# Queries through the hardware queues, wider warm-up matmuls and one PSUM tile less at the start of a sorted-attention and expert-layer kernel

## The chip, the core and the metric

The kernel runs on one core of a Trainium2 chip. TensorE (PE) multiplies matrices, VectorE (DVE), ScalarE (ACT) and GpSimd (POOL) work on vectors, SyncE (SP) issues transfers. The metric is the device time of one execution in microseconds. Three runs of the kernel before gave 359.15, 359.16 and 359.26 us, with a median of 359.16.

## The reference

Inputs: queries, keys and values of shape (4 batches, 8 heads, 768 positions, 64 features); a sort net of 8x8 numbers for each batch and head; expert weights w1 (4 experts, 512x1024) and w2 (4, 1024x512) and their probabilities for 3,072 tokens.

```python
P = sort_net
for _ in range(5):                      # alternating normalization
    P = exp(P - max(P))
    P = P / (sum(P, axis=-1) + 1e-9)
    P = P / (sum(P, axis=-2) + 1e-9)
k_sorted = einsum('bhij,bhjcd->bhicd', P, k_blocks)   # 8 blocks of 96 positions, mixed
v_sorted = einsum('bhij,bhjcd->bhicd', P, v_blocks)
attn = softmax(q_block @ k_sorted_block.T / 8)        # inside each block
x = attn @ v_sorted_block                             # to (3072 tokens, 512)
p = domain_probs / (sum(domain_probs) + 1e-9)
out = sum over e of p[:, e] * (relu(x @ w1[e]) @ w2[e])
```

## The kernel before

The work is written out by hand, in the order in which each engine is to take it; nothing reorders it. PSUM tiles come from pools that hand out two buffers in turn (`psM` and `psA`), so a tile waits until the one two before it in its pool has been read.

The start, which is all that the change touches, runs as follows. SP loads the sort net (L76) and the probabilities (L163). POOL issues, one after the other, the first half of the queries of batch 0 (two loads, L147), the keys and values of batch 0 in two groups of four heads (L110, cast from float32 to float16 on the way), the first expert's w1 (L134) and, between them, builds the identity matrix and masks. A query half is 64 positions of each row group; `half_queries` names it, `q0` holds it in float16.

PE meanwhile multiplies a constant tile (`dummy`, 128x128) by itself 84 times (`warm`, L260), transposes the first queries (`h_q`, L271, 48 matmuls) and multiplies `dummy` another 30 times.

The normalization loop (L283) is a chain between two engines: ACT's Exp (L284) on 32x64 numbers, then six DVE operations (two sums, two reciprocals, two products), five times. `p_steps` is a generator that normalizes the expert probabilities on DVE; each `next(p_steps)` (L301) puts one of its steps (sum, add, reciprocal, product with transfers) into DVE's order. At the last round DVE and POOL each expand one half of the normalized matrix into `sn16` (L304).

Then PE multiplies `sn16` by the identity (`r_half`, L316) into the PSUM tile `ps_R`, giving the matrix on all partitions. DVE builds the mixing operands `PI0` from it in two steps of four heads (`build_PI0`, L327). `mix_half` (L495, 24 matmuls for four heads, half of the output blocks) mixes keys or values into its own PSUM tile, after some matmuls on `dummy` (`keep_warm`, L481); `mixed` (L506) copies it out. `h_s` computes scores and their exponentials (L550, L556), `h_w` transposes values (L522), `h_a` applies the attention (L567), `h_x` transposes the result for the expert layer (L598), and `group0` (L679) is the first expert layer on it. Work of the first four heads (quad 0) and the second four (quad 1) is interleaved from L1365 on. `Rs` (L1372) is an SBUF copy of `ps_R`. From about 20 us on, PE works through the expert layers, with attention of later batches between them, to the end.

Of the kernel before, what the change touches and what calls it, by code (L numbers as in the profile page):

```python
# [9 lines left out]
F32 = mybir.dt.float32  # L10
F16 = mybir.dt.float16
# [6 lines left out]
def kernel(  # L18
# [11 lines left out]
    nc = tc.nc  # L30

    B, H, S, D = q.shape
    GH = B * H
# [5 lines left out]
    P = 128  # L39
# [3 lines left out]
    R = BLK // CP  # L43
    NKC = Dm // P
    NFC = FF // P
    NPB = H // 2
    HB = NB // 2
# [7 lines left out]
    const = ctx.enter_context(tc.tile_pool(name="const", bufs=1))  # L55
# [3 lines left out]
    psM = openM.enter_context(tc.tile_pool(name="psM", bufs=2, space=bass.MemoryType.PSUM))  # L59
# [5 lines left out]
    state = {"n": 0, "q": 0}  # L65

    def psa(shape, dtype, name):
        state["n"] += 1
        return psA.tile(shape, dtype, tag="ps", name=name)

    def psm(shape, dtype, name):
        return psM.tile(shape, dtype, tag="ps", name=name)
# [9 lines left out]
    Hflat = Hb.rearrange("p e f x -> p (e f x)")  # L82
# [12 lines left out]
    q0 = Tt[3].rearrange("p a f x -> p (a f x)").rearrange("p (f h r d) -> p f h r d", f=2, h=4, r=R)  # L95
# [7 lines left out]
    def half_queries(qd, hf):  # L103
        return q[0, ds(4 * qd, 4)].rearrange("h (p r) d -> p h (r d)", r=R)[ds(64 * hf, 64)]

    def load_natural(b, nm, qd):
        src = {"k": k, "v": v}[nm]
        t = arena[:, ds(("k", "v").index(nm) * 2 * NW + qd * NW, NW)].rearrange("p (h r d) -> p h r d", h=4, r=R)
        natural[(b, nm, qd)] = t
        nc.gpsimd.dma_start(  # L110
            t.rearrange("p h r d -> p h (r d)"),
            src[b, ds(4 * qd, 4)].rearrange("h (p r) d -> p h (r d)", r=R),
        )
# [9 lines left out]
    def head(b, nm, h):  # L123
        return natural[(b, nm, h // 4)][:, h % 4, :, :]

    w1sb, w2sb = [], []
# [4 lines left out]
    def load_w1(e, parts=1):  # L131
        n = NKC // parts
        for i in range(parts):
            nc.gpsimd.dma_start(  # L134
                w1sb[e][:, ds(i * n, n)], moe_w1[e].rearrange("(kc p) f -> p kc f", p=P)[:, ds(i * n, n)]
            )
# [8 lines left out]
    def load_half_queries(hf):  # L145
        for qd in range(2):
            nc.gpsimd.dma_start(  # L147
                q0[ds(64 * qd, 64), hf].rearrange("p h r d -> p h (r d)"), half_queries(qd, hf)
            )

    dummy = Hflat[:, ds(2 * NFC * 2 * P, P)]
    nc.vector.memset(dummy, 0.5)


# [2 lines left out]
    def p_part(at, n):  # L157
        return Tt[2].rearrange("p a f x -> p (a f x)")[:, ds(2 * at, 2 * n)].bitcast(F32)

    p_in = p_part(0, E * NT).rearrange("p (t e) -> p t e", e=E)  # L160
    p_out = p_part(E * NT, E * NT).rearrange("p (e t) -> p e t", e=E)
    p_den = p_part(2 * E * NT, NT).rearrange("p (t o) -> p t o", o=1)
    nc.sync.dma_start(p_in, moe_domain_probs.rearrange("(p t) e -> p t e", t=NT))  # L163
    load_half_queries(0)
    load_natural(0, "k", 0)


    ident = const.tile([P, P], F16, name="ident")
    make_identity(nc, ident)
    load_natural(0, "v", 0)  # L170
    load_natural(0, "k", 1)
    load_natural(0, "v", 1)
    load_w1(0, 2)

    eye16 = const.tile([P, CP], F16, name="eye16")
    maskk = const.tile([P, P], F16, name="maskk")
# [76 lines left out]
    qTs = {}  # L253
    q_ring = const.tile([P, 3, R, P], F16, name="q_ring")

    def warm(n):
        ps = psM.tile([P, 4, P], F32, tag="ps", name=f"ps_w_{state['n']}")
        state["n"] += 1
        for m in range(n):
            nc.tensor.matmul(ps[:, m % 4, :], dummy, dummy, start=True, stop=True)  # L260

    qT0 = [from_spare(2 * S).rearrange("p (s f r x) -> p s f r x", s=2, f=2, r=R) for _ in range(2)]

# [13 lines left out]
    srow = const.tile([GH, NB, 1], F32, name="srow")  # L277
    scol = const.tile([GH, NB, 1], F32, name="scol")
    sn16 = const.tile([GH, NB, NB, CP], F16, name="sn16")
    warm(84)  # L280
    p_steps = spread_weights()
    nc.gpsimd.tensor_copy(ident6, ident[0:R, 0:R])
    for it in range(5):  # L283
        nc.scalar.activation(sn[:], sn[:], AF.Exp, bias=0.0, scale=1.0)  # L284
        if it == 4:
            for qd in range(2):
                h_q(qd, 0, nc.scalar.copy)
            warm(30)
        nc.vector.tensor_reduce(srow[:], sn[:], AX.X, ALU.add)
        nc.vector.reciprocal(srow[:], srow[:])  # L290
        nc.vector.tensor_tensor(sn[:], sn[:], srow[:].broadcast_to([GH, NB, NB]), ALU.mult)
        nc.vector.tensor_reduce(scol[:], sn[:].rearrange("p i j -> p j i"), AX.X, ALU.add)
        nc.vector.reciprocal(scol[:], scol[:])
        if it < 4:
            nc.vector.tensor_tensor(
                sn[:], sn[:],
                scol[:].rearrange("p j o -> p o j").broadcast_to([GH, NB, NB]),
                ALU.mult,
            )
            if it:  # L300
                next(p_steps)  # L301

    for a, eng in enumerate((nc.vector, nc.gpsimd)):
# [4 lines left out]
            ALU.mult,  # L308
        )

    ps_R = psM.tile([P, 2, 512], F32, tag="ps", name="ps_R")
    Rv = ps_R[:, :, 0:HB * GH].rearrange("p a (i g) -> p a i g", g=GH)

    def r_half(a):
        for i in range(HB):
            nc.tensor.matmul(  # L316
                Rv[:, a, i, :], sn16[:, a * HB + i, :, :].rearrange("g j c -> g (j c)"),
                ident[0:GH, 0:GH], start=True, stop=True,
            )
# [155 lines left out]
    xsls0, xsl0 = {}, {}  # L475
    vT0 = {qd: from_spare(S) for qd in range(2)}

    def keep_warm(ps, n):

        for _ in range(n):  # L480
            nc.tensor.matmul(ps, dummy, dummy, start=True, stop=True)  # L481

    tails = {}

    def mix_half(nm, qd, hf, pool, warm_up=0):

        ps = pool([P, 1024], F32, f"ps_m{nm}_{qd}_{hf}")
        keep_warm(ps[:, 0:P], warm_up)
        tails[(nm, qd, hf)] = ps[:, 2 * R * 64:1024].bitcast(F16).rearrange("p (n x) -> p n x", n=2)
        ps = ps[:, 0:2 * R * 64].rearrange("p (s r x) -> p s r x", s=2, r=R)  # L490
        for sg in range(2):
            for r in range(R):
                for hh in range(2):
                    h = 4 * qd + 2 * sg + hh
                    nc.tensor.matmul(  # L495
                        ps[ds(D * hh, D), sg, r, :],
                        head(0, nm, h)[:, r, :],
                        PI0[hf][:, h, :, :].rearrange("p i c -> p (i c)"),
                        start=True, stop=True,
                    )  # L500
        return ps
# [38 lines left out]
    def h_s(qd, qq, ps=None):  # L540

        kT, ET = kTs[qd], ETs[2 * qd + qq % 2]
        if ps is None:
            ps = psa([P, 2, 512], F32, f"ps_s0_{qd}_{qq}")
        for n in range(4):
            for hh in range(2):
                sg, i = n // 2, 2 * (qq % 2) + n % 2

                m = BLK if 2 * i + sg == 3 else P
                nc.tensor.matmul(  # L550
                    ps[0:m, hh, ds(n * BLK, BLK)],
                    kT[ds(D * hh, D), ds((2 * i + sg) * BLK, m)],
                    qT0[qd][ds(D * hh, D), sg, qq // 2, :, ds((2 * (qq % 2) + n % 2) * CP, CP)],
                    start=True, stop=True,
                )
        nc.scalar.activation(  # L556
            ET[:, 0:S].rearrange("c (h x) -> c h x", h=2), ps[0:BLK, :, 0:HS],
            AF.Exp, bias=0.0, scale=SCALE,
        )
# [30 lines left out]
    def h_x(qq, copy, qds=range(2), ps=None, warm_up=0):  # L590

        nq = len(qds)
        if ps is None:
            ps = psa([P, 2, 512], F32, f"ps_x0_{qq}_{qds[0]}")
        keep_warm(ps[:, 0, 0:P], warm_up)
        for m, qd in enumerate(qds):
            for n in range(4):
                nc.tensor.matmul(  # L598
                    ps[:, m, ds(n * BLK, BLK)], xsl0[(qd, qq)][:, n, :, :].rearrange("c h d -> c (h d)"),
                    perm[:], start=True, stop=True,  # L600
                )
        copy(
            xTs[0][:, :, ds(2 * qq, 2), :].rearrange("p (q s) i x -> p q s (i x)", q=2)[:, ds(qds[0], nq)],
            ps[:, 0:nq, 0:4 * BLK].rearrange("p q (s x) -> p q s x", s=2),
        )
# [55 lines left out]

    def open_group(qq, g, warm_up=0):
        ps = groups[(qq, g)] = psm([P, 2, 512], F32, f"ps_h_0_{qq}_{g}")
        keep_warm(ps[:, 0, 0:P], warm_up)

    def group0(qq, nq, g, kcs=range(NKC), later=False):

# [5 lines left out]
        if (qq, g) not in groups:  # L673
            open_group(qq, g)
# [305 lines left out]
    for e in range(E):  # L980
        w, hk, hf = w1sb[e], NKC // 2, FF // 2
# [380 lines left out]
    ]  # L1362


    mk0 = mix_half("k", 0, 0, psm, 8)  # L1365
    mixed("k", 0, mk0, 0, 2, act)
    mv0 = mix_half("v", 0, 0, psa)
    mixed("v", 0, mv0, 0, 2, vec)
    h_s(0, 0)
    r_half(1)  # L1370
    mixed("k", 0, mk0, 2, 2, act)
    vec(Rs.rearrange("p g (a i) -> p a g i", a=2), Rv.rearrange("p a i g -> p a g i"))  # L1372
# [18 lines left out]
    h_w(1, vec, 0, 2, tails[("v", 1, 0)])  # L1391
    mixed("v", 1, mv1, 2, 2, act)
    ps_a10 = psa([P, 2, 512], F32, "ps_a10")
    keep_warm(ps_a10[:, 0, 0:P], 4)
    even01 = h_a(0, 1, ps_s01, True)
    h_a(1, 0, ps_a10)
    next(p_steps)
# [138 lines left out]
```

## Time and profile before

| What | Value |
|---|---|
| Median of three runs | 359.16 us (359.15 to 359.26) |
| Span of the profiled execution, first to last instruction | 357.8 us |
| Own time of the profiled execution | not given by the page; the median is 1.36 us above its span |
| PE busy, share of the span | 351.6 us, 98% |
| DVE, ACT, POOL busy | 276.2, 170.6, 133.6 us |
| Granted TensorE clock | 1.000 |
| HBM read, written | 42.13 MB, 6.34 MB |

The profile shows one execution. A chain of waits follows the work that ended last backwards, at each step to whatever released it. "Issue" in it is time in which an engine waited for nothing that the profile shows. In a timeline each line has a start, a duration (or the stretch of a merged group), the engine, the source line, the operation, the tiles and how many instructions were merged; in brackets stands the idle time before and who ended it. PEld is PE's weight load, one for every matmul.

### The profile page before, as it was taken

The page shows a single profiled execution, that of the slowest core. Times are in us where ns is not written, and L with a number is a line of the kernel's source. Part 1 is how long each engine was busy: PE and PEld are TensorE (multiplying, and loading weights), DVE is VectorE, ACT ScalarE, POOL GpSimd, SP SyncE. Part 2 cuts the span into 40 slices and gives each one's busy share as a digit, 9 for nine tenths or more (in the row PEclk, how much of TensorE's full clock was granted, in tenths as well). Part 3 has the DMA queues.
Part 4 walks back from the last instruction along what each step waited for, and adds up shares of the span by engine and source line. Part 5 has one row for each costly group of instructions (what it writes and reads, how often), then busy time and mean ns, then how long its engine had stood idle before and what let it go on. Part 6 is the DMA issues. An engine that isn't in the chain of part 4 may idle for free.

```text
span 357.8 us, 9498 instructions
## 1 busy us (share of the span) xinstructions
PE 351.6 (98%) x3949; PEld 306.3 (86%) x3949; DVE 276.2 (77%) x552; ACT 170.6 (48%) x303; POOL 133.6 (37%) x149
## 2 busy tenths in 40 slices
PE   8899999999999999999999999999999999999996
PEld 8686867888888888888899988888888888888886
DVE  5754797869889587868978988896678886588963
ACT  2554240442434535367947258830288611688201
POOL 8864010375122222000535318840058800188400
PEclk9999999999999999999999999999999999999999
DMA  8999999999999999935996420005200015100011
GB/s 114 207 205 228 216 210 198 209 163 165 201 154 160 188 152 170 194 74 73 168 201 90 102 78 0 2 2 108 102 29 2 3 39 138 61 0 2 2 73 46
DMA packets 72022, 40.51 MB, mean 113 GB/s; under 512 B 40614, under 2 KB 66732, under 8 KB 71980
## 3 DMA queue, kind: packets, MB, share of 16 engines
q0 software_dynamic: 36576, 19.93, 41.9%
q1 hardware_dynamic: 35260, 19.92, 28.5%
q8 instruction: 31, 0.51, 0.6%
q14 instruction: 11, 0.09, 0.1%
q10 hardware_dynamic: 144, 0.07, 0.1%
HBM read 42.13 MB, written 6.34 MB: 135 GB/s over the span
## 4 chain that ended last, share of the span: by engine, by line
PE 95%; DVE 2%; ACT 1%; DMA 0%; issue 0%; DVEq 0%
PE ps_h L790 18%; PE ps_Q L1264 18%; PE ps_p L774 12%; PE ps_X L1121 10%; PE ps_Z L1121 7%; PE ps_Q L1121 7%; PE ps_Z L1264 6%; PE ps_h L679 3%; PE ps_o L714 3%; PE ps_p L830 3%; PE ps_a L453 2%; PE ps_s L418 2%; PE ps_k L399 1%; PE ps_v L365 1%; PE ps_a L567 1%; PE ps_mk L495 1%
## 5 line engine op out<-in xcount | busy, mean ns | idle before, releaser
L790 PE MATMUL ps_h<-xT,w 128*128 128x256 f16 x576 | 67.5, 273 | 0.0
L790 PEld LDWEIGHTS <-w 128*128 128x128 f16 x576 | 55.2, 98 | 7.2
L796 DVE SCALAR_TENSOR_TENSOR Hb<-ps_h,pb 128x1024 f16<-128x1024 f32 x34 | 41.5, 1223 | 17.2 <-PE ps_h L790 15.8
L1121 PEld LDWEIGHTS <-w 128*128 128x128 f16 x480 | 43.6, 98 | 4.8
L1134 POOL TENSOR_TENSOR arena<-tmp,pb 128x512 f16<-128x512 f32 x12 | 15.2, 1275 | 65.7 <-PE ps_Z L1121 49.8
L1264 PEld LDWEIGHTS <-Hb 128*128 128x128 f16 x320 | 31.1, 98 | 3.5
L1133 ACT ACTIVATE tmp<-tmp 128x512 f32<-128x512 f32 x46 | 29.0, 632 | 3.9 <-DVE tmp L1171 3.9
L1264 PEld LDWEIGHTS <-Sb 128*128 128x128 f16 x304 | 28.3, 98 | 3.0
L1121 PEld LDWEIGHTS <-arena 128*128 128x128 f16 x312 | 27.7, 98 | 2.9
L425 ACT ACTIVATE ET<-ps_s 96x768 f16<-96x768 f32 x24 | 18.0, 802 | 25.1 <-PE ps_s L418 24.8
L121 POOL DMA_DIRECT2D arena<-in_q_dram x24 | 19.9, 838 | 25.5 <-DMA q_ring<-arena 25.2
L408 ACT CAST kT<-ps_k 64x384 f16<-64x384 f32 x48 | 22.7, 473 | 13.3 <-PE ps_k L399 12.3
L1121 PE MATMUL ps_X<-ET,arena 128*128 128x256 f16 x168 | 25.2, 272 | 0.0
L1264 PE MATMUL ps_Q<-w,Hb 128*128 128x256 f16 x192 | 24.6, 273 | 0.0
L774 PEld LDWEIGHTS <-Hb 128*128 128x128 f16 x232 | 21.8, 98 | 3.0
L1127 DVE SCALAR_TENSOR_TENSOR Hb<-ps_X,pb 128x512 f16<-128x512 f32 x27 | 18.7, 691 | 7.0 <-PE ps_X L1121 7.0
L1141 ACT COPY ps_X<-ps_Z 128x512 f32<-128x512 f32 x27 | 15.4, 571 | 17.8 <-PE ps_Z L1121 17.8
L1121 PE MATMUL ps_Z<-xT,w 128*128 128x256 f16 (+1 forms) x176 | 22.5, 258 | 0.0
L760 DVE TENSOR_TENSOR Sb<-Hb 128x512 f16<-128x512 f16 x33 | 20.6, 647 | 0.0
L1148 ACT COPY tmp<-ps_X 128x512 f32<-128x512 f32 x26 | 15.2, 585 | 9.2 <-PE ps_X L1121 6.6
L1127 DVE SCALAR_TENSOR_TENSOR Hb<-ps_Z,pb 128x512 f16<-128x512 f32 x27 | 18.4, 682 | 1.3 <-PE ps_Z L1121 1.3
L1171 DVE TENSOR_TENSOR tmp<-ps_Q,tmp 128x512 f32<-128x512 f32 x26 | 17.8, 683 | 0.8 <-PE ps_Q L1121 0.8
(266 smaller groups left out, 741.6 us busy)
## 6 DMA issues: line engine op xcount, KB each, us to landing
w<-in_moe_w_dram POOLq DMA_DIRECT2D x6, 1024.0 KB, 27.9
pb<-p_dram SPq DMA_DIRECT2D x9, 512.0 KB, 7.0
arena<-in_k_dram POOLq DMA_DIRECT2D x8, 384.0 KB, 9.3
arena<-in_v_dram POOLq DMA_DIRECT2D x8, 384.0 KB, 7.5
vs<-arena SPq DMA_DIRECT2D x36, 66.0 KB, 4.9
arena<-in_q_dram POOLq DMA_DIRECT2D x24, 96.0 KB, 7.5
out_dram<-ob SPq DMA_DIRECT2D x9, 256.0 KB, 2.0
w<-in_moe_w_dram POOLq DMA_DIRECT2D x4, 512.0 KB, 12.5
```

The costliest lines, as they stand in the source:

```text
L121: nc.gpsimd.dma_start(t[:, h // 2, :, h % 2, :], q[b, h].rearrange("(t p) d -> p t d", p=P))
L408: nc.scalar.copy(kT[ds(D * hh, D), r], pk[ds(D * r, D), hh].rearrange("p a (i c) -> p a i c", c=CP),)
L425: nc.scalar.activation(ETs[2 * (pr % 2) + hh][:, 0:S].rearrange("c (a x) -> c a x", a=2), pss[hh][0:BLK, :, 0:HS], AF.Exp, bias=0.0, scale ...
L760: tt(sm[0], blk(0, 1), blk(1, 1), ALU.add)
L774: nc.tensor.matmul(ps, lhs(e, f), Ts[e][rhs][:, f, :], start=(first and e == es[0] and f == 0), stop=(done and e == es[-1] and f == KH - 1 ...
L790: nc.tensor.matmul(ps[:, f, :], w1sb[e][:, kc, ds((4 * g + f) * P, P)], xT[:, kc, ds(2 * c * P, 2 * P)], start=(kc == 0), stop=(kc == NKC ...
L796: nc.vector.scalar_tensor_tensor(out=Hb[:, homes.get(e, e), ds(4 * g, 4), :], in0=ps[:], scalar=0.0, op0=ALU.max, in1=weights(e).broadcast ...
L1121: nc.tensor.matmul(dst[:, ds(f * cols, cols)], a[lhs][:, k, ds((f0 + f) * P, P)], t[rhs][:, k, :], start=(first and f == 0 and k == 0), st ...
L1127: nc.vector.scalar_tensor_tensor(out=home(i, j), in0=src.rearrange("p (f x) -> p f x", f=m), scalar=0.0, op0=ALU.max, in1=weight(j).broadc ...
L1133: nc.scalar.activation(src, src, AF.Relu, bias=0.0, scale=1.0)
L1171: tt(t12, Q, u2, ALU.add)
L1264: nc.tensor.matmul(ps, lhs(e, f), Ts[e][rhs][:, f, part], start=(first and e == 0 and f == 0), stop=(e == E - 1 and f == KH - 1), skip_gro ...
```

## The change

Six edits are made together.

1. The first half of the queries of batch 0 is loaded as float32, one half of the heads by SP's queue and the other by ACT's, into a part of the room of the first expert's w2. ACT casts it into `q0` in two copies, in rounds 2 and 3 of the normalization loop (counted from 0), behind the Exp. POOL no longer issues these loads; the loads of keys, values and w1 come first on POOL, and the identity is made after them.
2. `dummy` has 512 columns, and a warm-up matmul multiplies its first 128 columns by all 512: 21 in place of 84, 8 in place of 30, 2 in place of 8 before the key mix, 1 in place of 4 before `ps_a10` is used.
3. `ps_R` is a tile of 1,024 columns, with the sort matrices in its last 256, and the first key mix takes the first 768 of the same tile in place of a tile of its own.
4. As `mix_half` takes no tile for that mix, later tiles of `psM` move by one buffer.
5. The first step of `p_steps` moves from round 1 to round 2, the second from 2 to 3, and the third, a reciprocal, from round 3 to behind the first `h_s`.
6. `keep_warm` is defined earlier, and `warm` calls it.

```diff
-    dummy = Hflat[:, ds(2 * NFC * 2 * P, P)]
+    dummy = Hflat[:, ds(2 * NFC * 2 * P, 512)]
...
+    q32 = w2sb[0].rearrange("p f d -> p (f d)").bitcast(F32)[:, 0:4 * R * D].rearrange("p (h x) -> p h x", h=4)
+    for qd, queue in enumerate((nc.sync, nc.scalar)):
+        queue.dma_start(q32[ds(64 * qd, 64)], half_queries(qd, 0))
     nc.sync.dma_start(p_in, moe_domain_probs.rearrange("(p t) e -> p t e", t=NT))
-    load_half_queries(0)
     load_natural(0, "k", 0)
-    ident = const.tile([P, P], F16, name="ident")
-    make_identity(nc, ident)
     load_natural(0, "v", 0)
     load_natural(0, "k", 1)
     load_natural(0, "v", 1)
     load_w1(0, 2)
+    ident = const.tile([P, P], F16, name="ident")
+    make_identity(nc, ident)
...
+    def keep_warm(ps, n):
+        for _ in range(n):
+            nc.tensor.matmul(ps, dummy[:, 0:P], dummy, start=True, stop=True)
     def warm(n):
-        ps = psM.tile([P, 4, P], F32, tag="ps", name=f"ps_w_{state['n']}")
+        ps = psM.tile([P, 512], F32, tag="ps", name=f"ps_w_{state['n']}")
         state["n"] += 1
-        for m in range(n):
-            nc.tensor.matmul(ps[:, m % 4, :], dummy, dummy, start=True, stop=True)
+        keep_warm(ps[:], n)
...
-    warm(84)
+    warm(21)
     for it in range(5):
         nc.scalar.activation(sn[:], sn[:], AF.Exp, bias=0.0, scale=1.0)
+        if it in (2, 3):
+            nc.scalar.copy(
+                q0[:, 0, ds(2 * (it - 2), 2)].rearrange("p h r d -> p h (r d)"), q32[:, ds(2 * (it - 2), 2)]
+            )
         if it == 4:
             for qd in range(2):
                 h_q(qd, 0, nc.scalar.copy)
-            warm(30)
+            warm(8)
...
-            if it:
+            if it > 1:
                 next(p_steps)
...
-    ps_R = psM.tile([P, 2, 512], F32, tag="ps", name="ps_R")
-    Rv = ps_R[:, :, 0:HB * GH].rearrange("p a (i g) -> p a i g", g=GH)
+    ps_R = psM.tile([P, 1024], F32, tag="ps", name="ps_R")
+    Rv = ps_R[:, 2 * R * 64:1024].rearrange("p (a i g) -> p a i g", a=2, g=GH)
...
-    def mix_half(nm, qd, hf, pool, warm_up=0):
-        ps = pool([P, 1024], F32, f"ps_m{nm}_{qd}_{hf}")
-        keep_warm(ps[:, 0:P], warm_up)
+    def mix_half(nm, qd, hf, pool, warm_up=0, ps=None):
+        if ps is None:
+            ps = pool([P, 1024], F32, f"ps_m{nm}_{qd}_{hf}")
+        keep_warm(ps[:, 0:512], warm_up)
...
-    mk0 = mix_half("k", 0, 0, psm, 8)
+    mk0 = mix_half("k", 0, 0, psm, 2, ps_R)
     mixed("k", 0, mk0, 0, 2, act)
     mv0 = mix_half("v", 0, 0, psa)
     mixed("v", 0, mv0, 0, 2, vec)
     h_s(0, 0)
+    next(p_steps)
     r_half(1)
...
-    keep_warm(ps_a10[:, 0, 0:P], 4)
+    keep_warm(ps_a10[:, 0, :], 1)
```

## The prediction

> **What bounds the kernel now.** I read the page's engine line, queues and chain first, then the chain of waits and the timeline of the first 32 us, which the change touches.
>
> ```profile
> span 357.8 us, 9498 instructions
> PE 351.6 (98%) x3949; PEld 306.3 (86%) x3949; DVE 276.2 (77%) x552; ACT 170.6 (48%) x303; POOL 133.6 (37%) x149
> ...
> q8 instruction: 31, 0.51, 0.6%
> ...
> PE 95%; DVE 2%; ACT 1%; DMA 0%; issue 0%; DVEq 0%
> ```
>
> TensorE (PE) carries 95% of the chain. Nothing in the diff alters its real work, so only a shift of the moment when it becomes continuously busy counts. The chain of waits of the start (start, us, what):
>
> ```profile
> 0.74 1.71 DMA sn<-in_sort_net_dram
> ...
> 2.47 0.27 ACT sn L284
> ...
> 11.06 0.69 DVE sn L304
> ...
> 12.64 0.58 PE ps_mk L495 x24
> ...
> 13.99 0.18 issue
> ...
> 14.73 0.43 DVE Rs L1372
> ...
> 18.95 0.40 PE ps_a L567 x8
> ...
> 20.07 0.20 issue
> ```
>
> The sort net's load starts five rounds of Exp (ACT) and six DVE operations, 1.77 us a round; TensorE's warm-up and the loads lie beside them. From 11.79 the chain runs through PE, ACT and DVE in turn, and from 20.3 it stays on PE. Two "issue" pieces stand in it. The timeline shows them as stops inside a group of equal matmuls, where no engine is waited for:
>
> ```profile
> 9.43 0.28 DVE L235 RECIPROCAL T<-T 128x24 f32<-128x24 f32 x1
> 12.17 0.75 DVE L327 TENSOR_TENSOR Sb<-maskk,ps_R 128x256 f16<-128x256 f16 x2 [0.43 <-PE ps_R L316]
> 13.78 0.21 PE L550 MATMUL ps_s<-Sb,kT 64*128 64x96 f16 x1 [0.19 <-ACT kT L506]
> 14.17 0.33 PE L550 MATMUL ps_s<-Sb,kT 64*128 64x96 f16 x7 [0.18 <-issue]
> 17.50 0.35 PE L550 MATMUL ps_s<-Sb,kT 64*128 64x96 f16 x8
> 19.85 0.22 PE L522 MATMUL ps_s<-ident,Sb 128*96 128x128 f16 x1
> 20.27 0.37 PE L522 MATMUL ps_s<-ident,Sb 128*96 128x128 f16 x3 [0.20 <-issue]
> ```
>
> Each of these matmuls started about 0.4 us after the one before (13.78 to 14.17, 19.85 to 20.27). Counting weight load and matmul pairs in the timeline from the start (84, 48, 30, 4, 8, 24, 24, ...), the stops fall at the 224th and the 352nd pair: 128 pairs, or 256 instructions, apart. The instruction queue moved 31 packets of 0.51 MB in all, 16 KB each, and PE's 7,898 instructions make 31 blocks of 256. So I read the stops as PE reaching a block that had not arrived. The DMA view has refills starting at 11.79, 17.86 and 23.89 us, each 2.4 us before such a block is used (14.17, 20.27); the block after 20.27 follows 6.1 us behind the one before.
>
> **The change, part by part.**
>
> *Start.* ScalarE now issues a query load ahead of its table load. SyncE's two first loads were issued 0.47 us apart, so the table load moves from 0.74 to 1.21 and ends at 2.49, against the Exp's start at 2.47: +0.04. The two query loads also share the DMA engines with the sort net's last packets: between 0 and 0.25 us (three of the 84 ns that a 2,048 B packet of the hardware queue takes in the trace). A gain is excluded, since the sort net's landing sets the start. I take +0.1 for both, with ends 0 and 0.3, near the low end because the probabilities' 48 KB, right behind the sort net, landed in 1.8 us beside its 1.7.
>
> *Query loads and casts.* POOL loses two query issues (1.4 us), so key, value and w1 issues and the masks come earlier; nothing waits for them today (masks done by 9.9, used at 12.17). Two casts of 128x768 enter ScalarE behind the third and fourth Exp (6.02, 7.78). The row of 128x768 casts from PSUM says 0.81 (L506), 128x512 from SBUF 0.63 (L1133): 0.85 each, inside the 1.5 us that ScalarE idles there. Cost 0 while the queries land before 6.9. Before, the same queries landed at 5.9 (issued at 2.08, 3.8 to landing); now they are issued by 1.3. The DMA engines do almost nothing else until 2.6. PE's first transposes wait for the second cast (8.9), end near 9.6, and the second warm-up near 11.4, ahead of the 11.79 at which the sort matrices arrive. The probabilities, now behind a query load, are first needed at 7.7.
>
> *Warm-ups.* 84 matmuls took 7.2 us; 21 of four times the columns are the same columns. Ends: 5.1 us at the 0.243 us of a 512-column matmul (L714, four in 0.97) and 9.0 if the slow first phase (107 ns per 128 columns until 5.9) lasted throughout; at 9.0 the second warm-up would end 1.1 us too late. The slow phase ended after 4.9 us of steady matmuls, which these are too, so I take 7.2 and 0. The larger memset (0.17 us for 128 columns) delays only PE's start. The two matmuls ahead of the key mix take 0.49 against 0.45 for eight, with 0.2 us of slack before DVE's first build; cost 0.
>
> *Reciprocal.* It leaves its place beside the fifth Exp for the stretch before the Rs copy. DVE is idle there from 14.19 to 14.73, and it takes 0.28: 0 as things stand, but if Rs could start earlier, it would be next in the way, at 14.5.
>
> *Shared tile.* The key mix's last eight pairs now write the PSUM bank from which DVE's second build reads until 12.92. Ends: 0 (no wait drawn) and 0.4 (all 24 pairs wait for it). If only the eight wait, they start at 12.96 instead of 12.9: +0.06, taken since only those touch that bank. The next key mix no longer waits for Rs (0.16), but the group after it waits for DVE anyway: 0.
>
> *Fewer PE instructions.* Up to the key mix, 91 pairs go (63+22+6), later 3 more. The stops leave their places. Without them: the first group of scores ends 0.37 earlier, Rs is held by the reciprocal (-0.22), the chain through DVE runs 0.22 to 0.3 early up to the transposes at 20.4, and the second stop no longer adds: -0.3 in all. Ends: -0.73 (both stops in full) and 0. The boundaries now fall at the 96th pair, inside the key mix, and the 224th, the fifth of the eight pairs at 17.50, which would run at 17.4. Is the block there in time? The refill at 11.79 delivered at 14.17. Near 200 us a refill started at 198.60 whose boundary PE crossed at 200.27, so PE's front end asks at least 1.67 us, 31 instructions of 55 ns, ahead; adding the 1.7 us that a small load takes to land, up to 62. With 62 ahead the old request came at 6.95 and took 7.2 us; the new one comes at 9.5 (the transposes) and delivers at 16.7: no stop. With 31 ahead: 11.85 and 6.3, delivering at 18.15; with none, 12.85 and 5.8, at 18.65. I take 0, because the 1.67 us must also hold the transfer's own start-up, which puts it nearer 62.
>
> The Trainium skill, "Runtime: NRT & Kernel Launch", section "Instruction fetch mechanics", says that code comes in 16 KiB blocks of 256 instructions and that crossing into one is mostly hidden. The trace agrees on the 256, and shows two crossings that were not hidden, 0.4 us each. By the page alone moving them is worth nothing, and the sum would be +0.16, 359.3. "TensorE: Matmul & The Clock Gate" of the Trainium skill, in its opening table, gives PE a queue of 64 instructions; this speaks for the 62.
>
> *Sum:* +0.10 +0.06 -0.30 = -0.14 us. The span is 357.8; the runs' median, 359.16, is 1.36 more, which I take as lying outside the first and last instruction and unchanged. 359.16 - 0.14 = 359.0.
>
> **Rivals.**
>
> 1. *The refill comes too late at the new place* (slower). If PE's front end doesn't run ahead past the wait in front of the key mix, the request comes at 12.85 and delivers between 18.65 and 18.9 (6.1 later). Scores of the second quad, its transposes and PE's h_a at 18.95 all follow: the -0.3 becomes +0.75 to +1.0, in sum +0.9 to +1.2, 360.2. It exceeds 0.2% from a delivery at 18.5 on. For it: the refills of 14.17 and 20.27 left no slack. Against it: the 1.67 us.
> 2. *A crossing costs its 0.4 us itself*, or the refill is half late (18.15). Then the key mix pays about 0.35 at its 13th pair, the fifth pair at 17.50 pays up to 0.38, and the chain through DVE keeps about 0.4 of it: 359.6. For it: both stops measure the same. Against it: the third crossing, near 26.8, shows none.
> 3. *The queries come late.* If they share the engines evenly with the first key load, they land when both did before, at 8.9; the first cast sits in front of Exp, and the chain slips by up to 2.0: 359.9 to 361.0. Against it: idle DMA engines until 2.6.
> 4. *More is recovered*: the reciprocal and the start cost nothing and both stops return in full: 358.4.
>
> **How the numbers follow.** Forecast 359.0 (358.7 to 359.5): 0.60. Rival 2, 359.6: 0.17. Rival 1: 0.12. Rival 3: 0.05. Rival 4 and other gains: 0.06. A difference within 0.2%, 0.72 us, is about what can't be told from no change. Faster than 358.44: 0.05. Slower than 359.88: rivals 1 and 3, 0.17, and 0.02 from the edges of the others: 0.19. Same: 0.76. The range goes from 358.5, which leaves out part of rival 4, to 360.0, which leaves out rivals 1 and 3.
>
> **What would show it.** First Exp at 2.5 to 2.6; Exps 1.77 apart, with a cast of 0.85 in two gaps; the key mix near 12.7, its pairs without a break; no "issue" piece near 14 or 20; Rs near 14.6; PE continuous from about 20.1. A break among the eight pairs at 17.4 is rival 1, at the mix's 13th pair rival 2, a longer gap between the third and fourth Exp rival 3. A refill's start near 14.4 would show the run-ahead, one at 15.8 or later would not.

## The result, and the profile after

The changed kernel took 362.13 us (median of six runs, 361.67 to 369.63), the kernel before 359.19 us beside it. The ratio is 1.0076, with an interval of 1.0058 to 1.0094. The forecast was 359.0, with a range up to 360.0: the change makes the kernel about 3 us slower, outside the range.

The first execution of the changed kernel that was profiled was a long one (369.63 us), of a kind told of at the end. The profile read here is that of an execution of 362.91 us, of the run `whole_again`. The page's first lines, its instruction queue and the shares of its chain of waits:

```profile
span 361.1 us, 9316 instructions
PE 351.1 (97%) x3855; PEld 300.1 (83%) x3855; DVE 276.4 (77%) x552; ACT 172.0 (48%) x305; POOL 132.3 (37%) x147
...
q8 instruction: 30, 0.49, 0.6%
...
PE 88%; DMA 5%; SPq 2%; DVE 2%; ACT 1%; issue 1%; ACTq 0%; DVEq 0%
```

PE has as much work as before (351.1 against 351.6 us), 94 matmuls fewer, and one block of instructions fewer. The chain has lost 7 points on PE, and transfers have gained as much (DMA 5, SPq 2). Of the DMA share the page puts 2% on the load of the probabilities at the start and 3% on a later transfer, `vs`. The timeline shows the start (start, duration, engine, line, operation, tiles; in brackets the idle time before and who ended it):

```profile
0.74 0.71 ACTq L165 DMA_DIRECT2D w<-in_q_dram  x1
1.20 0.75 SPq L165 DMA_DIRECT2D w<-in_q_dram  x1
2.77 0.26 ACT L289 ACTIVATE sn<-sn 32x64 f32<-32x64 f32 x1
7.71 0.83 ACT L291 CAST T<-w 128x768 f16<-128x768 f32 x1 [1.16 <-DMA w<-in_q_dram]
8.45 0.25 ACT L289 ACTIVATE sn<-sn 32x64 f32<-32x64 f32 x1
8.57 0.25 DVE L232 TENSOR_REDUCE T<-T 128x24 f32<-128x96 f32 x1 [0.37 <-DMA T<-in_moe_domain_probs_dram]
11.73 0.68 DVE L313 TENSOR_TENSOR sn<-sn,scol 32x512 f16<-32x512 f32 x1
13.64 0.59 PE L260 MATMUL ps_R<-Hb 128*128 128x512 f16 x2 [0.92 <-DVE Sb L336]
14.16 0.57 PE L500 MATMUL ps_R<-Sb,arena 128*64 128x64 f16 x24
16.40 0.47 ACT L511 CAST kT<-ps_R 128x384 f16<-128x384 f32 x1
16.90 0.43 DVE L1378 CAST Rs<-ps_R 128x256 f16<-128x256 f32 x1 [0.98 <-ACT kT L511]
```

Four waits are new. ACT's first cast waits for the queries, and the Exp of the same engine stands behind it. DVE's sum waits for the probabilities. And two waits stand on the shared tile `ps_R`: the warm-up matmuls wait for DVE's builds, and the copy `Rs` waits for ACT's second key copy. No "issue" stop inside a group of equal matmuls is left, as forecast.

A second profile of the kernel before belongs beside these, of an execution of 359.16 us, exactly the median (`before_again`). Its timeline at the same steps:

```profile
2.39 0.26 ACT L284 ACTIVATE sn<-sn 32x64 f32<-32x64 f32 x1 [0.36 <-DMA sn<-in_sort_net_dram]
11.06 0.68 DVE L304 TENSOR_TENSOR sn<-sn,scol 32x512 f16<-32x512 f32 x1
12.64 0.57 PE L495 MATMUL ps_mk<-Sb,arena 128*64 128x64 f16 x24
13.78 0.35 PE L550 MATMUL ps_s<-Sb,kT 64*128 64x96 f16 x8 [0.19 <-ACT kT L506]
14.36 0.42 DVE L1372 CAST Rs<-ps_R 128x256 f16<-128x256 f32 x1 [0.17 <-PE ps_R L316]
```

The eight score matmuls at 13.78 run without the stop that the first profile shows inside them. The two code-block stops that the forecast meant to recover are not in this execution, whose time is the median. Its span is 357.4 us, so 1.76 us lie outside the span; the first profile (span 357.8) was then of an execution of about 359.6 us, 0.4 above the median.

Against this median execution the changed kernel is late by

| Step | before (us) | after (us) | late |
|---|---|---|---|
| first Exp | 2.39 | 2.77 | 0.38 |
| product `sn16` | 11.06 | 11.73 | 0.67 |
| key mix | 12.64 | 14.16 | 1.52 |
| `Rs` | 14.36 | 16.90 | 2.54 |
| PE at 26 us | | | 2.45 |
| last matmul | | | 3.86 |

The last two rows compare the start of the same matmul, counted from the end of the program. 1.41 us are added after 26 us: 0.35 near 164, 0.79 at 182 and 0.27 at 266 us. The fastest runs (361.67) are 2.5 above the kernel before, which would be the start's loss alone; none of them was profiled.

### The profile page after: what moved, and what is told of

The parts are those of the page before. It is cut to its first block, busy times and chain, and to the rows that moved or that the text cites. A ratio compares the mean times of both kernels' runs of the same rounds, so it can differ in the third digit from the quotient of the medians.

```text
span 367.8 us, 9316 instructions
## 1 busy us (share of the span) xinstructions
PE 356.1 (97%) x3855; PEld 304.4 (83%) x3855; DVE 280.8 (76%) x552; ACT 172.4 (47%) x305; POOL 132.4 (36%) x147
## 4 chain that ended last, share of the span: by engine, by line
PE 93%; DVE 3%; DMA 2%; ACT 1%; issue 0%; SPq 0%; ACTq 0%; DVEq 0%
PE ps_h L795 17%; PE ps_Q L1269 17%; PE ps_p L779 12%; PE ps_X L1126 10%; PE ps_Z L1126 6%; PE ps_Q L1126 6%; PE ps_Z L1269 6%; PE ps_o L719 3%; PE ps_h L684 3%; PE ps_p L835 3%; DMA T<-in_moe_domain_probs_dram 2%; PE ps_a L462 2%; PE ps_s L427 2%; DVE T L238 1%; PE ps_k L408 1%; PE ps_v L374 1%
## 5 line engine op out<-in xcount | busy, mean ns | idle before, releaser
L779 PEld LDWEIGHTS <-Hb 128*128 128x128 f16 x232 | 21.8, 98 | 3.0
```

The source lines that it names most:

```text
L779: nc.tensor.matmul(ps, lhs(e, f), Ts[e][rhs][:, f, :], start=(first and e == es[0] and f == 0), stop=(done and e == es[-1] and f == KH - 1 ...
```

## The experiments

"Late at 26 us" is in all of them PE's lag behind `before_again`, in the one profiled execution; the first profile of before has 0.46 by this measure, its two stops. Times are medians, beside the kernel before on the same chip (359.4 to 359.6).

**The change as a whole and by its parts.** `whole_again` is the change unaltered. The parts, each put alone into the kernel before:

```diff
# tile_only
+    ps_R = psM.tile([P, 1024], F32, tag="ps", name="ps_R")
+    mk0 = mix_half("k", 0, 0, psm, 8, ps_R)
# loads_only: loads, casts, POOL's order, moved p_steps
+        queue.dma_start(q32[ds(64 * qd, 64)], half_queries(qd, 0))
# warm_only
+    dummy = Hflat[:, ds(2 * NFC * 2 * P, 512)]
+    warm(21)
```

> The changed kernel as it is, for a profile with an undisturbed TensorE clock. All theories expect 361.7 to 363.1 us, as in its first runs. Theory T (the shared PSUM tile carries it): sort matrices (L313) near 11.8 (+0.7 against before), first warm-up matmul on ps_R only after DVE's second build, Rs only after ScalarE's second key copy, so Rs near 17 (14.73 before). Theory L (the loads carry it): most of the shift is already there at L313, over 1.5 us. Theory K (the code refill or the clock carries it): a break of over 0.5 us inside a group of equal matmuls, or a clock below 1 after the second warm-up.

> The kernel before with the shared PSUM tile alone (sort matrices and first key mix in one tile). Theory T: the matmuls on the tile wait for both DVE builds (+0.7 to +0.9) and the Rs copy waits for ScalarE's second key copy (+0.6 to +1.0); 360.7 to 361.2 us. Theories L and K: at most +0.3, 359.0 to 359.5 us.

> The kernel before with the float32 query loads, the two ScalarE casts, the new order of POOL's loads and the moved probability steps; warm-ups and tiles as before. Theory T: +0.7 (first Exp 0.3 late behind the ScalarE issue, then the first cast and the probabilities' sum wait for their loads), 359.7 to 360.1 us. Theory L: +2 or more, over 361.0 us. Theory K: between 359.2 and 359.9 us.

> The kernel before with warm-up matmuls of 512 columns alone (21, 8, 2 and 1 of them). Theories T and L: the two stops near 14 and 20 us go and nothing comes in their place, 358.7 to 359.1 us; a refill of code starts near 14.4. Theory K: a stop appears in the fifth of the eight matmul pairs near 17.4, or the clock falls; over 359.9 us.

| Run | Time | Ratio (interval) | Profiled execution | Late at 26 us | Added later |
|---|---|---|---|---|---|
| whole_again | 362.41 | 1.0081 (1.0064 to 1.0097) | 362.91 | 2.45 | 1.41 |
| tile_only | 362.44 | 1.0067 (1.0046 to 1.0088) | 361.06 | 1.80 | 0.00 |
| loads_only | 360.35 | 1.0025 (1.0007 to 1.0043) | 359.82 | 0.66 | 0.06 |
| warm_only | 361.29 | 1.0054 (1.0035 to 1.0072) | 360.70 | 0.99 | 0.55 |

Loads and tile together give 0.66 + 1.80 = 2.46, the 2.45 of the whole. The tile's two waits in `tile_only`:

```profile
12.98 0.61 PE L481 MATMUL ps_R<-Hb 128*128 128x128 f16 x8 [0.92 <-DVE Sb L327]
16.25 0.42 DVE L1373 CAST Rs<-ps_R 128x256 f16<-128x256 f32 x1 [1.19 <-ACT kT L507]
```

This sum holds for single executions at 26 us. By the medians `tile_only` alone is 2.88 above the kernel before, as much as the whole change (2.85): its profile is of one of its two fastest executions, and the four others took 362.09 to 368.77 us. What made those longer was not profiled and is not shown.

The warm-ups cost 0.99 alone, and the sum leaves nothing for them in the whole. The chain of `warm_only` shows what the 0.99 is:

```profile
17.19 0.19 PE ps_s L549 x4
17.38 0.99 issue
18.37 0.26 PE ps_s L549 x4
```

PE stops inside the eight pairs, at the fifth, for the block of instructions that the boundary inside the key mix asked for. PE crossed that boundary at 12.82, the block's packets started at 16.15 and ended at 17.10, and its first instruction ran at 18.37. This is rival 1, at its place and 0.3 us earlier than it said. In the whole the boundary is crossed at 14.37, because the tile's wait holds the key mix, and the fifth pair runs at 19.63, 1.71 us after the block's packets have ended: the tile's wait covers the stop.

**Which part covers which.** `no_tile` is the change without the shared tile; `no_tile_84` is the same with the first 84 narrow warm-ups back; `late_wide` is the kernel before with only the later warm-ups wide; `tile_rs_first` is `tile_only` with the copy `Rs` put ahead of ACT's second key copy.

```diff
# no_tile (from the change)
+    ps_R = psM.tile([P, 2, 512], F32, tag="ps", name="ps_R")
+    mk0 = mix_half("k", 0, 0, psm, 2)
# no_tile_84 (from no_tile) and late_wide (from before, warm-ups wide)
+    for m in range(84):
+        nc.tensor.matmul(ps_n[:, m % 4, :], dummy[:, 0:P], dummy[:, 0:P], start=True, stop=True)
# tile_rs_first (from tile_only)
+    vec(Rs.rearrange("p g (a i) -> p a g i", a=2), Rv.rearrange("p a i g -> p a g i"))
     mixed("k", 0, mk0, 2, 2, act)
-    vec(Rs.rearrange("p g (a i) -> p a g i", a=2), Rv.rearrange("p a i g -> p a g i"))
```

> The changed kernel without the shared tile: the first key mix has its own PSUM tile again, everything else stays changed. Theory T (the tile's waits carry the loss): they go, and 2.0 of the 2.9 us come back, +0.8 against the kernel before. Theory M (the parts cover one another): without the tile's waits PE reaches the fifth pair of the eight score matmuls before its code does, and waits about 1 us there near 18 to 19; +2.0 to +2.5 against the kernel before, nearly as slow as the whole change.

> As no_tile, but with the first warm-up of 84 matmuls of 128 columns again (the later warm-ups stay wide). PE then passes its 192nd instruction in the transposes near 8.7 and the next block is asked for 4 us sooner. Theory M: no stop at any block boundary before 26 us; +0.1 to +0.5 against the kernel before. Theory T, in which the number of PE instructions doesn't matter: the same as no_tile.

> The kernel before, with the first warm-up as it was and only the later ones wide (8, 2 and 1 of 512 columns in place of 30, 8 and 4 of 128). The boundaries move 28 and 31 pairs to later work, the first request stays at 8.4. Theory M: both stops (near 14 and 20 us) go and none comes, -0.2 to -0.4 against the kernel before. Rival: a crossing costs 0.4 us wherever it falls, the stops reappear at the later places; -0.1 to +0.2.

> tile_only with one line moved: the Rs copy on DVE is put ahead of ScalarE's second copy of the key mix, so it no longer has that copy's reading of the same tile in front of it. If the Rs wait carries the tile's loss: Rs starts near 15.2 instead of 16.3, and about 1 us comes back, +0.5 to +1.0 against the kernel before. If the wait of the tile's matmuls for both builds carries it: less than 0.4 comes back.

| Run | Time | Ratio (interval) | Profiled execution | Late at 26 us | Added later |
|---|---|---|---|---|---|
| no_tile | 361.83 | 1.0055 (1.0037 to 1.0073) | 362.44 | 3.06 | 0.32 |
| no_tile_84 | 360.15 | 1.0015 (1.0003 to 1.0026) | 360.09 | 0.63 | 0.00 |
| late_wide | 359.93 | 1.0012 (1.0000 to 1.0025) | 361.05 | 0.47 | 1.42 |
| tile_rs_first | 360.68 | 1.0029 (1.0015 to 1.0042) | 360.76 | 0.89 | 0.55 |

Without the tile the stop comes out, and longer, as the key mix now starts late too; the chain of `no_tile`:

```profile
17.93 0.19 PE ps_s L555 x4
18.12 1.29 issue
19.42 0.26 PE ps_s L555 x4
```

Behind this stop PE's granted clock fell to 0.50 (20 to 22 us), which is part of the 3.06. With the first warm-ups narrow (`no_tile_84`) the boundary falls elsewhere, and what is left, 0.63, is about the 0.66 of the loads. So the wide first warm-up costs through where the block boundary comes to lie. `late_wide` lost its stops but for one of 0.16 us, and was not faster. In `tile_rs_first` the copy `Rs` no longer waits for ACT:

```profile
15.31 0.42 DVE L1372 CAST Rs<-ps_R 128x256 f16<-128x256 f32 x1 [0.24 <-PE ps_R L316]
```

`tile_only` had it at 16.25 and `before_again` at 14.36: in these profiles the order of two copies is half of the tile's loss (0.89 against 1.80).

**The three waits by themselves.** `p_first` loads the probabilities ahead of the queries on SP; `tile_free` is `tile_rs_first` with the eight warm-ups of the key mix moved ahead of the sort matrices; `sp_late` is a version meant to keep what was good: no query load on ACT, casts one round later, narrow first warm-up, the eight later ones ahead of the query transposes, no shared tile.

```diff
# p_first (from loads_only)
+    nc.sync.dma_start(p_in, moe_domain_probs.rearrange("(p t) e -> p t e", t=NT))
     for qd, queue in enumerate((nc.sync, nc.scalar)):
         queue.dma_start(q32[ds(64 * qd, 64)], half_queries(qd, 0))
-    nc.sync.dma_start(p_in, moe_domain_probs.rearrange("(p t) e -> p t e", t=NT))
# tile_free (from tile_rs_first)
-            warm(30)
+            warm(38)
-    mk0 = mix_half("k", 0, 0, psm, 8, ps_R)
+    mk0 = mix_half("k", 0, 0, psm, 0, ps_R)
# sp_late (from late_wide, with POOL's order of the change)
     nc.sync.dma_start(p_in, moe_domain_probs.rearrange("(p t) e -> p t e", t=NT))
-    load_half_queries(0)
+    for qd in range(2):
+        nc.sync.dma_start(q32[ds(64 * qd, 64)], half_queries(qd, 0))
...
+        if it in (3, 4):
...
+            warm(8)
             for qd in range(2):
                 h_q(qd, 0, nc.scalar.copy)
-            warm(8)
```

> This is the kernel before with the query loads, the casts, POOL's order and the moved steps, as in the run loads_only, but the probabilities are loaded by SyncE ahead of its query load. Theory W (the probabilities' late landing, behind a query load on the same queue, costs most of the 0.67 us by which the product sn16 came late): they land near 3.5 us, the sum on DVE no longer waits at 8.57, only the first cast still waits for the queries (7.7) and holds the fourth Exp by at most what remains; sn16 at 11.2 to 11.5 in place of 11.73. Rival C (the first cast alone holds the chain, since it stands behind the third Exp and ahead of the fourth): the fourth Exp stays at 8.45 or later, as the query load of SyncE is now issued 0.5 us later, and sn16 comes at 11.7 to 12.2. Either way the two stops of PE on its code blocks near 14.4 and 20.4 us stay, and take up what is won, so that the time is 359.3 to 360.4 under both.

> This is the kernel before with the shared tile, the copy Rs ahead of ScalarE's second key copy, and the eight warm-up matmuls of the key mix put behind the thirty at the end of the normalization, so that PE's count of instructions is that of before. Theory T (the tile costs by its two waits and by nothing else: the warm-ups and the mix wait for both of DVE's builds, and Rs waits for the second key copy): the mix starts at about 12.98, when the second build ends, in place of 12.64 before and 13.5 with the warm-ups behind that wait; the scores follow at 14.13, Rs near 14.8; the time is that of before plus 0 to 0.3 us. If something else is at work in the tile (the bank shared by PE's writes and DVE's reads, or the tiles of the pool that move by one buffer), the time stays near the 360.7 us of the run with Rs first.

> This is a version without the waits found so far: the kernel before with the wide later warm-up matmuls (the first 84 stay narrow), POOL's order of the change (keys, values and w1 issued earlier), the queries as float32 on SyncE's queue alone and behind the probabilities, so that ScalarE issues no load ahead of its table load, the casts one round later (behind the fourth and the fifth Exp), and the thirty warm-up matmuls ahead of the query transposes; the sort matrices have their own tile. If ScalarE's issue, the cast that came too early and the probabilities' place were all that the loads cost, the first Exp is at 2.47, the Exps are 1.77 apart, sn16 is at 11.06, and PE's stops at 14 and 20 us are gone. If the landing of w1's second half (21.65 us) was the next cover in the run late_wide, its earlier issue by POOL lets PE gain up to 0.5 us there: 358.6 to 359.0, against the 359.2 to 359.5 of the kernel before. If the time stays at that of before or above, another cover lies behind w1, or the query loads cost on.

`tile_free` took 360.34 us (1.0028, 1.0015 to 1.0041); its mix started at 12.99, `Rs` at 14.77, and PE was 0.35 late at 26 us, where `tile_only` had 1.80. At 26 us the tile's two waits are thus nearly all of its loss; 0.47 more came later, 0.40 of it where DVE waited for a transfer (`pb`) near 98 us. The time misses the 0 to 0.3 us that were expected: its median is 0.93 above the kernel before, that of `tile_rs_first` 1.23. So the two waits are shown for the start, and what the tile costs beyond it, its moved buffers among the candidates, stays open.

`p_first` and `sp_late` came out no faster than the whole change (1.0081): 362.36 (1.0085, 1.007 to 1.01) and 363.60 (1.015, 1.011 to 1.019). Rival C held, and more strongly than it was put. ACT's timeline of `p_first`, and then that of `sp_late`:

```profile
9.10 0.83 ACT L288 CAST T<-w 128x768 f16<-128x768 f32 x1 [2.53 <-DMA w<-in_q_dram]
9.84 0.25 ACT L286 ACTIVATE sn<-sn 32x64 f32<-32x64 f32 x1
```

```profile
10.76 0.83 ACT L294 CAST T<-w 128x768 f16<-128x768 f32 x1 [2.56 <-DMA w<-in_q_dram]
11.50 0.25 ACT L292 ACTIVATE sn<-sn 32x64 f32<-32x64 f32 x1
```

The last query load of SP is issued at 1.20 in the whole change, at 1.66 in `p_first` and near 2.4 in `sp_late`; the queries were there at 7.7, 9.0 and 10.7. About half a microsecond later in the queue goes with 1.3 in the landing. By 1.3 us POOL has begun to issue the keys, so that the transfers share the engines is the likely reason, not tested by itself. The loads' 0.66 was then a good case, made so by the place ahead of all other traffic.

**What is left: the covers behind, and the late waits.** `w1_early` is `late_wide` with w1 issued 0.6 us earlier by POOL; `shift` is the kernel before with ten small copies on ACT ahead of its first Exp; `whole_third` and `before_again` repeat the two kernels unaltered.

```diff
# w1_early (from late_wide)
-    ident = const.tile([P, P], F16, name="ident")
-    make_identity(nc, ident)
     load_natural(0, "v", 0)
...
     load_w1(0, 2)
+    ident = const.tile([P, P], F16, name="ident")
+    make_identity(nc, ident)
# shift (from before)
+    for n in range(10):
+        nc.scalar.copy(Hflat[:, ds((2 * NFC * 2 + 1) * P, P)], dummy)
```

> This is the kernel before with the later warm-up matmuls wide and, on POOL, the loads of keys, values and w1 all ahead of the identity; queries, probabilities and the sort tile as before. The run late_wide had its two code-block stops almost gone, and PE was 0.28 us early up to 21.4 us, but there it waited 0.28 us for w1's second half, which landed at 21.65. If that landing is the cover that took the gain, w1 is asked for about 0.7 us earlier here, lands about as much earlier, and PE keeps 0.2 to 0.4 us: 358.9 to 359.3 where the kernel before gives 359.4. If w1's landing is set by the DMA engines and not by its issue, or if the next cover lies right behind, the time stays at late_wide's 359.9 or at that of before.

> This is the kernel before with ten copies of 128x128 on ScalarE ahead of its first Exp, so that the chain of the start begins about 2.0 us later (first Exp near 4.5) while every load is issued at the same time as before; nothing else is changed. Theory S (the late waits of the changed kernel, at 164, 182 and 266 us, come from the start's delay against the transfers): PE is 1.6 to 2.1 us late at 25 us and loses 0.3 to 1.5 us more at waits for transfers later; the time is 361.8 to 362.9. Theory Z (such waits come by chance in some executions, whatever the kernel): PE is 1.6 to 2.1 us late at 25 us and stays so, with the fastest of its times at 361.0 to 361.3, and the kernel before shows such waits in some executions as well.

> This is the changed kernel, once more. Its last profile lost 1.99 us by 25 us and 1.4 us more at three waits of PE and ACT for transfers (v in front of PE's second attention product at 182 us, another at 164, one near 266). Theory S (they belong to the change): the same waits come back at the same places, of a size near 0.3 to 0.8 us each. Theory Z (chance): the offset at 25 us is 1.9 to 2.1 again, and the later waits are elsewhere, of another size, or absent.

> This is the kernel before, once more, for a second profile. Theory Z (late waits for transfers come by chance): some execution of it shows a late wait of 0.3 us or more too, since its times on these chips reach from 359.1 to 360.5. Theory S: its offsets from the first profile stay within 0.1 us to the end. Under both its two stops of PE at 14 and 20 us come back at the same instructions, of about 0.4 us each.

`w1_early` took 359.89 us (1.0009, 0.9999 to 1.0019): no gain. PE still waited for w1's second half, and longer than in `late_wide` (0.28 there), as the timeline has it:

```profile
21.87 0.83 PE L680 MATMUL ps_h<-xT,w 128*128 128x192 f16 x8 [0.65 <-DMA w<-in_moe_w_dram]
```

Issued earlier, it landed no earlier (21.8 against 21.65); from 8 to 28 us the queues move some 180 to 215 GB/s in both kernels. That w1 is bound by this rate is argued from those rows, not tested by itself. If it is, PE cannot be more than some tenths of a microsecond earlier at 22 us, however the start is arranged.

`shift` took 365.14 us (1.0178, 1.0135 to 1.0222; four runs, 363.61 to 368.09). The copies took 0.33 us each, not the 0.2 assumed, so `sn16` came 2.9 late; PE was 4.57 late at 26 us and stayed so to the end. This profile, of one of its two faster executions (363.72), gives theory S, that a late start brings late waits for transfers, no support. The extra 1.7 us at the start are put down to the clock (below).

`whole_third` lost time at the same places as `whole_again`, some 6 us later on its own time axis: 0.60 us where ACT's copy waits for `vs` near 170, 0.39 at 188, and 0.27 at 272. `before_again` showed none. Theory Z, chance alone, does not fit that well either. The wait at 182 us came in four of the five profiled executions with 94 matmuls fewer and one of the four with 31 fewer, and in none of the eight with the count of before. Something in the fewer instructions goes with it; what, these runs do not settle. The 0.27 at 266 us came in all three executions of the whole change and in no other kernel, and has no releaser in the profile. Both stay open; they are at most 1.4 of some 3 us in the profiled executions.

No version beat the kernel before.

## Why the prediction was wrong, point by point

The forecast was -0.14 us, the measured change +2.94. The term that was wrong by most is the wait on the shared tile: put at +0.06, it made PE 1.80 us late in `tile_only`. The loads, +0.10 in the sum, made 0.66, and the -0.30 was not there. Together that is the 2.45 of the start; the rest came later and stays open.

- **Shared tile, +0.06: 1.80.** The step read a wait as drawn for the columns that overlap. It is drawn for the tile: the warm-ups, in the first 512 columns, waited for builds that read the last 256 columns, and `Rs`, which reads those columns, waited for ACT's copy of others. The upper end of 0.4 was too low too, as it looked at the mix and not at `Rs` behind it. At `Rs` the text looked only for a gain, the next key mix that no longer waits for it.
- **Fewer PE instructions, -0.30: 0.** The step that failed is the base of the sum. The two stops of 0.4 us were read from one execution and taken for a property of the kernel, but the second profile, of an execution at the median, doesn't have them, so there was nothing to recover. The text set the span of 357.8 against the median and called the 1.36 us between them what lies outside the span; it is 1.76 (359.16 less 357.4), and the missing 0.4 was the stops. Two things differ between the profiles. PE crosses the first boundary at 8.37 or 7.67, as the slow first phase of the warm-ups ends at 6.03 in the first profile and at 4.55 in `before_again`; and the refill's packets start 3.42 or 2.72 us behind that crossing, for no reason that is seen. The next block is needed at 13.78 in both.
- **Run-ahead of 62 instructions: not at the start.** At the first three boundaries of the seventeen profiles the refill's packets start 2.5 to 4.2 us after PE itself has crossed, in 48 of 51 cases, and a stopped PE goes on 1.3 to 1.5 us after they end. From one boundary to a stopped start of the next block that makes 5.5 to 6.2 us. The distance near 200 us was read rightly: in the first profile, with PE's semaphore instructions counted too, eleven of the last twelve refills start 0.1 to 1.8 us before PE reaches the boundary (198.60 against 200.38). The step carried it over to the start, where PE waits for another engine every few matmuls. That these waits hold the run-ahead back is argued from the rows, not tested by itself; `sp_late` has a little of it past a wait (packets at 11.09, while PE waits until 11.64, three pairs ahead of the boundary). The 12.85 and 18.65 of rival 1 were measured as 12.82 and 18.37 in `warm_only`, where it had the mechanism, the place and the size (0.99). In the change itself its stop did not come, as the tile's wait covered it. The Trainium skill's "Runtime: NRT & Kernel Launch", section "Instruction fetch mechanics", says that a crossing is mostly hidden; here two were not: 1.19 us between the two matmuls in `warm_only` and 1.49 in `no_tile`.
- **Start, +0.10: 0.38 of 0.67.** ACT's issue of the query load took 0.71 us, not the 0.47 between SP's two small ones; the table load followed at 1.48. Against a first Exp at 2.39 that is 0.38.
- **Queries and casts, 0: the other 0.29.** The landing was put before 6.9, from loads of another queue (5.9 before); it was 7.7. The cast in front of the Exp is rival 3, in a mild form; `p_first`, 2.97 late at 26 us, shows it in full. The probabilities, "first needed at 7.7", landed at 8.55: they were moved behind a load, and that was priced at nothing.
- **Warm-ups, 0: right as to time** (the first 21 took 6.12 us in `whole_again`, between the ends of 5.1 and 9.0), wrong as to where the boundary goes.
- **Reciprocal, 0: right** (15.63, beside ACT's Exp). **Rival 2 fell**: boundaries crossed with the block at hand show no break (19.63 in `whole_again`). **Rival 4** had nothing to recover, and w1 stands behind it.
- Of what was to show it, the first Exp (2.5 to 2.6), the spacing of the Exps, the mix near 12.7, `Rs` near 14.6 and PE continuous from 20.1 all failed. The absence of "issue" pieces held, but by luck: without the tile's wait, in `no_tile`, the stop is there.

## What to carry to other kernels

Before a stop seen in one profile is booked as a gain, set that execution's own time against the median: if it is slower by as much as the stop, the stop isn't in the median. When two uses are put into one tile, list every instruction that touches any part of it, and reckon that each may wait for all the others; and when the number of instructions changes, find where the block boundaries fall in time, as a stop that is hidden today moves with them.

## What the runs showed of the hardware

**PE's clock falls after a pause.** In `shift` PE has nothing to do from 10.7 to 14.7 us. The windows view (stretch, then for each engine busy time and count, the granted clock, the DMA share and GB/s):

```profile
12.00:14.00 2.00, 0.00 (x0) 0.00 (x0) 1.69 (x9) 1.55 (x3) 0.00 (x0) 1.00 1.32 201
14.00:16.00 2.00, 1.26 (x39) 1.17 (x41) 1.39 (x3) 0.07 (x1) 1.99 (x2) 0.99 1.19 212
16.00:18.00 2.00, 2.00 (x47) 1.63 (x41) 0.98 (x2) 1.21 (x3) 2.00 (x4) 0.50 1.13 212
...
20.00:22.00 2.00, 2.00 (x45) 1.56 (x42) 1.25 (x3) 1.23 (x2) 2.00 (x5) 0.50 1.29 199
```

The clock is 0.50 from 16 to 22 us and PE is busy all that time: a pause of 4 us costs a second time. `p_first` (0.50 from 12 to 14) and `sp_late` (12 to 18) show it after their late queries, behind pauses of 2.6 and 1.9 us. "TensorE: Matmul & The Clock Gate" of the Trainium skill, under "What's actually happening", gives half the clock after an idle window of about 3.4 us, free-running and so different from run to run; the trace agrees on the half, and the slow first phase of the warm-ups ended anywhere from 4.1 to 7.1 us here, but the two shorter pauses show that PE need not be idle for all of 3.4 us.

**The changed kernel sometimes runs long.** Two of its eleven executions took 369.63 and 369.1 us; of the 84 executions of the kernel before that ran beside these kernels none was above 361.0. `tile_only` (368.77), `sp_late` (367.28, 367.92) and `shift` (366.56, 368.09) had long executions too, of which none was profiled; the two of the changed kernel were. In both the clock falls behind the waits on the tile, and DVE's product of the probabilities, pushed from 19.86 (`before_again`) to 23.59 and 23.26, meets POOL's four builds; the timeline of `whole_third`, DVE and then POOL:

```profile
23.26 4.79 DVE L238 TENSOR_TENSOR T<-T 128x96 f32<-128x96 f32 x1
```

```profile
23.78 1.09 POOL L355 TENSOR_TENSOR arena<-maskv,Rs 128x512 f16<-128x512 f16 x1
...
26.80 1.06 POOL L347 TENSOR_TENSOR arena<-maskk,Rs 128x512 f16<-128x512 f16 x1
```

A product that took 0.31 us in `whole_again` takes 4.79 and ends 0.2 us behind POOL's last build; PE stands still from 26 to 28 us. "SBUF — State Buffer" of the Trainium skill, section "Who interferes with whom", states that a DVE instruction with two SBUF inputs and a GpSimd instruction that reads SBUF shut each other out; the trace agrees, 4.79 us against 0.31. In `whole_again` the product came at 22.31, 1.4 us ahead of the builds. That the fall of the clock is what delays it in the long executions is read from two profiles, and not tested by itself.

**A query load takes longer to issue than the sort net.** In `whole_again` ACT and SP took 0.71 and 0.75 us to issue one query load (384 KB) each, and SP 0.40 for the sort net (8 KB). What sets this is not shown: the probabilities (48 KB) took 0.59 there and 0.41 in `p_first`. Ahead of a table load it is time on the path.
